# Retention and a gated MLP on one core: the first two blocks re-ordered

## The chip, the core and the metric

The kernel runs on one core of one Trainium2 chip. A core has five engines with queues of their own, each in program order: TensorE (PE, matrix products), VectorE (DVE), ScalarE (ACT), GpSimd (POOL) and SyncE (SP, which here only issues DMAs). They wait for each other through semaphores. PE writes to PSUM, which has eight banks of 128 partitions x 512 float32. The metric is the device time of one execution, in microseconds (us), median of several runs.

## What is computed

```python
# q, k, v: (8 batches, 8 heads, 576 positions, 64)
scores = q @ k^T / sqrt(64)
Dmat   = gamma_h ** (i - j) for i >= j, else 0      # gamma_h = 1 - 2**(-5-h)
attn   = (scores * Dmat) @ v
x      = attn, as 4608 tokens x 512                  # 8 * 576 tokens
h      = x @ w_in                                    # 512 x 2048
g      = h * cos(h)
out    = g @ w_out                                   # 2048 x 512, float32
```

## The kernel before

The attention is done per batch in five chunks r = 0..4 of 128 positions (the last has 64), the MLP in nine blocks j of 512 tokens. Batches have 576 tokens and blocks 512, so block 0 lies wholly in batch 0, and block 1 takes batch 0's last 64 tokens and the first 448 of batch 1.

**One chunk.** Three loads on SP's queue bring k, q and v (256 KB each; 128 KB in the last chunk) into float32 tiles kn, qn, vn. There is one set of these tiles, so the load of batch b+1's chunk r waits until the casts of batch b's chunk r have read them. The casts make bf16: `kcast` copies k, `decay` multiplies q and v by powers of gamma. `turn` transposes k and q by four matmuls each against the identity, into a PSUM bank, and ACT copies the bank to the tile kqt (L286). From batch 2 on `prep_dma` does the casts on POOL and the transposition by a DMA on SP instead. `scores` multiplies (banks sc0 and sc1), and DVE applies the mask (L325). `rest` gives the chunk's output in bank po and the running state in bank st, and ACT copies po to the token store xt (L367) and st to sb (L371).

**One block.** `mlp1(j, dt, o0, n)` computes 128 columns of the first layer for n tokens: four matmuls into one of four banks mm0 to mm3, taken in turn by `bank`; ACT takes the cosine as a shifted sine (L389), DVE multiplies (L392) into the tile gt. `mlp2(j, st, part)` does a quarter of the second layer's contraction for 128 tokens; after four parts ACT copies the bank to one of three float32 buffers osb (L414), and a DMA on SP stores it (L416). An osb buffer is written again only when its store has landed.

**Order.** The order of each queue is the order in which `emit` writes the calls. SP loads chunks 0 to 3 of batch 0. POOL issues the four loads of w_in (each 512 KB as stored in bf16), the first three held until q of chunk 1, 2 and 3 has landed, then four loads of w_out; SP's load of chunk 4 is held until the second of w_in has landed. In batch 0 ACT casts k, DVE decays q and POOL decays v, behind its weight loads. `idle` issues matmuls on a zero tile. Block 0's first layer is done partly in groups of 256 tokens, as chunks come. Then, for each block, the second layer's sixteen calls run with token tile st outside and part inside, so that one bank finishes every fourth call; between them stand the rest and the scores of the next batch, and in block 0 also the casts and turns of batch 1 with the loads of batch 2. From block 1 on, the first layer runs with `prep_dma` of batch j+1 between its groups, each followed by the loads of batch j+2.

## Time and profile before

| | us |
|---|---|
| runs | 338.02, 337.24, 331.56 (median 337.24) |
| the profiled execution | 334.09 |
| its span, first to last instruction | 332.4 |
| PE busy | 302.3 (91%) |
| ACT busy | 182.8 (55%) |
| DVE busy | 152.2 (46%) |
| POOL busy | 105.4 (32%) |

### The profile page before, as it was taken

How to read it: one execution, taken by the hardware profiler on the slowest of the kernel's cores; microseconds unless marked ns; L12 is line 12 of the kernel's file. 1: busy time of each engine (PE TensorE's matmuls, PEld its weight loads, DVE VectorE, ACT ScalarE, POOL GpSimd, SP SyncE). 2: the span in 40 equal slices, each digit the busy share in tenths (PEclk: the TensorE clock that was granted, in tenths of full speed). 3: DMA queues.
4: the chain of work that ended last, by engine and by line, in shares of the span. 5: the costliest groups of instructions: out<-in, count | busy, mean ns of one | idle time of the engine just before them, and what ended most of it. 6: DMA issues, size and time to landing. Idle time of an engine off the chain costs nothing.

```text
span 332.4 us, 5974 instructions
## 1 busy us (share of the span) xinstructions
PE 302.3 (91%) x2271; PEld 154.7 (47%) x2310; DVE 152.2 (46%) x244; ACT 182.8 (55%) x336; POOL 105.4 (32%) x125
## 2 busy tenths in 40 slices
PE   6219669999999999999999999999999999999996
PEld 2106444555445445544554455445544554444442
DVE  2205457334843574357335833574367427604710
ACT  8206677566734773477347744764376447625721
POOL 1272177763546064506540535055400000000000
PEclk9756799999999999999999999999999999999999
DMA  9999999986996599569946995799480100011002
GB/s 170 225 209 194 211 207 198 230 195 144 221 201 173 126 219 201 162 133 233 193 140 150 204 196 150 163 213 190 133 165 10 64 33 32 4 63 63 2 37 89
DMA packets 150556, 49.41 MB, mean 149 GB/s; under 512 B 141824, under 2 KB 145920, under 8 KB 150528
## 3 DMA queue, kind: packets, MB, share of 16 engines
q1 hardware_dynamic: 146304, 44.84, 64.6%
q0 software_dynamic: 4224, 4.19, 7.6%
q8 instruction: 18, 0.29, 0.4%
q14 instruction: 10, 0.08, 0.1%
HBM read 36.70 MB, written 9.44 MB: 139 GB/s over the span
## 4 chain that ended last, share of the span: by engine, by line
PE 89%; SPq 3%; DMA 2%; issue 2%; POOL 2%; ACT 2%; DVE 0%; ACTq 0%
PE mm L300 57%; PE mm L302 20%; PE po L300 6%; PE sc L300 4%; SPq L225 3%; DMA qn<-in_q_dram 2%; PE st L300 1%; POOL wout L238 1%; POOL win L231 0%; ACT xt L367 0%; ACT osb L414 0%; ACT kqt L286 0%; POOL vb L253 0%; DVE kq L253 0%; ACT sb L371 0%
## 5 line engine op out<-in xcount | busy, mean ns | idle before, releaser
L392 DVE TENSOR_TENSOR gt<-mm,cb 128x512 bf16<-128x512 f32 (+1 forms) x152 | 100.5, 664 | 61.6 <-ACT cb L389 60.3
L300 PE MATMUL mm<-xt,win 128*128 128x512 bf16 (+1 forms) x443 | 116.1, 371 | 1.1 <-ACT xt L367 0.6
L389 ACT ACTIVATE cb<-mm,c_pih 128x512 bf16<-128x512 f32 (+1 forms) x152 | 100.6, 665 | 29.6 <-PE mm L302 29.0
L300 PE MATMUL mm<-wout,gt 128*128 128x512 bf16 x407 | 111.6, 380 | 2.6 <-issue 2.5
L325 DVE TENSOR_TENSOR rt<-sc,mk 128x512 bf16<-128x512 f32 (+1 forms) x80 | 47.2, 631 | 99.0 <-PE sc L302 99.0
L300 PEld LDWEIGHTS mm<-xt,win 128*128 128x128 bf16 x456 | 44.7, 99 | 50.4 <-ACT xt L367 0.7
L300 PEld LDWEIGHTS mm<-wout,gt 128*128 128x128 bf16 x432 | 39.0, 98 | 45.1 <-issue 0.4
L302 PE MATMUL mm<-xt,win 128*128 128x512 bf16 (+1 forms) x152 | 56.4, 371 | 0.4
L302 PE MATMUL mm<-wout,gt 128*128 128x512 bf16 x144 | 54.6, 379 | 0.5
L367 ACT ACTIVATE xt<-po 128x512 bf16<-128x512 f32 (+1 forms) x40 | 22.2, 555 | 57.1 <-PE po L302 57.0
L414 ACT ACTIVATE osb<-mm 128x512 f32<-128x512 f32 x36 | 21.5, 597 | 51.7 <-PE mm L302 51.7
L246 POOL CAST kq<-kn 128x512 bf16<-128x512 f32 (+1 forms) x35 | 21.3, 610 | 80.7 <-DMA kn<-in_k_dram 69.5
L253 POOL TENSOR_TENSOR vb<-vn,wv 128x512 bf16<-128x512 f32 (+1 forms) x40 | 41.9, 1054 | 12.6 <-DMA vn<-in_v_dram 12.2
L253 POOL TENSOR_TENSOR kq<-qn,uq 128x512 bf16<-128x512 f32 (+1 forms) x35 | 36.5, 1042 | 22.6 <-DMA qn<-in_q_dram 22.6
L300 PE MATMUL po<-rt,vb 128*64 128x128 bf16 (+1 forms) x280 | 16.1, 225 | 12.8 <-POOL vb L253 12.8
L371 ACT ACTIVATE sb<-st 64x256 bf16<-64x256 f32 x64 | 23.9, 373 | 0.8
L302 PEld LDWEIGHTS mm<-xt,win 128*128 128x128 bf16 x152 | 15.0, 99 | 16.4
L302 PEld LDWEIGHTS mm<-wout,gt 128*128 128x128 bf16 x144 | 14.1, 98 | 17.0
L300 PEld LDWEIGHTS po<-rt,vb 128*64 128x64 bf16 (+1 forms) x280 | 9.8, 110 | 18.9 <-POOL vb L253 13.0
L300 PE MATMUL sc<-kqt 64*128 64x128 bf16 (+1 forms) x280 | 15.7, 221 | 1.9 <-ACT kqt L286 1.9
L286 ACT ACTIVATE kqt<-mm 128x512 bf16<-128x512 f32 (+1 forms) x20 | 10.3, 553 | 6.8 <-PE mm L302 6.6
L300 PEld LDWEIGHTS po<-kqt,sb 128*128 128x128 bf16 x128 | 9.6, 100 | 6.9
(40 smaller groups left out, 122.9 us busy)
## 6 DMA issues: line engine op xcount, KB each, us to landing
out_dram<-osb SPq DMA_DIRECT2D x36, 256.0 KB, 2.2
kn<-in_k_dram SPq DMA_DIRECT2D x32, 256.0 KB, 4.0
qn<-in_q_dram SPq DMA_DIRECT2D x32, 256.0 KB, 4.6
vn<-in_v_dram SPq DMA_DIRECT2D x32, 256.0 KB, 4.7
win<-in_moe_w_in_dram POOLq DMA_DIRECT2D x4, 512.0 KB, 7.2
wout<-in_moe_w_out_dram POOLq DMA_DIRECT2D x4, 512.0 KB, 15.4
kn<-in_k_dram SPq DMA_DIRECT2D x8, 128.0 KB, 3.1
qn<-in_q_dram SPq DMA_DIRECT2D x8, 128.0 KB, 3.7
```

Of the source, the lines that this page charges most:

```text
L225: return self.s.dma("sp", f"{x}n{r}", lambda e: e.dma_start(dst, src), writes=[bt], after=after)
L246: fn = (lambda e: e.activation(o, x, AF.Copy)) if eng == "act" else (lambda e: e.tensor_copy(o, x))
L253: self.s.op(eng, lambda e: e.tensor_tensor(bass.AP(t, off, [[pitch, ck], [D_, H_], [1, D_]]), bass.AP(self.ST32[x][r], 0, [[DM, ck], [D_, ...
L286: fn = (lambda e: e.activation(o, p, AF.Copy)) if eng == "act" else (lambda e: e.tensor_copy(o, p))
L300: self.nc.tensor.matmul(o, a, b, **kw)
L302: return s.done("pe", self.nc.tensor.matmul(o, a, b, **kw), reads, writes)
L325: s.op("dve", lambda e: e.tensor_tensor(bass.AP(self.RT[r % 2][hp], 0, p3), bass.AP(self.SC[hp], 0, p3), bass.AP(self.MK, 0, [[CH, ck], [0 ...
L367: fn = (lambda e: e.activation(o, p, AF.Copy)) if xeng == "act" else (lambda e: e.tensor_copy(o, p))
L371: s.op("act", lambda e: e.activation(bass.AP(self.SB[r % 2], 64 * hp * 512 + 64 * hp, [[512, 64], [128, NP], [1, D_]]), bass.AP(self.ST, 6 ...
L389: s.op("act", lambda e: e.activation(ci, mi, AF.Sin, bias=self.C_PIH.ap(), scale=1.0), reads=[bm, self.bC], writes=[bcb])
L392: s.op("dve", lambda e: e.tensor_tensor(bass.AP(g, dt * TB + o0, [[16 * TB, 128], [1, n]]), mi, ci, ALU.mult), reads=[bm, bcb], writes=[bg])
L414: s.op("act", lambda e: e.activation(o.ap(), m.ap(), AF.Copy), reads=[bm], writes=[bo])
```

## The change

Batch 0's casts: k on ACT, q and v on DVE. SP loads all five chunks of batch 0 at once. POOL's weight loads are held for k of chunk 2 and of chunk 3; only two of w_out's four loads stand ahead, the other two behind POOL's casts of batch 1's chunk 0. Chunk 4's scores and rest stand within block 0's first layer. All casts of batch 1, each with the loads of batch 2, stand ahead of block 0's second layer. That layer runs with part outside and token tile inside, in the four mm banks at once, and batch 1's turns then use the banks sc0 and sc1. Block 1's first layer runs in three strips of 192, 128 and 192 tokens, with batch 1's remaining turns, scores and rests and batch 2's `prep_dma` between the groups.

```diff
-    def turn(self, b, r, x, eng):
+    def turn(self, b, r, x, eng, sc=None):
...
-        m, bm = self.bank()
+        m, bm = self.bank() if sc is None else (self.SC[sc], self.bSC[sc])
...
-    def mlp2(self, j, st, part):
+    def mlp2(self, j, st, part, wide=False):
...
-        if part == 0:
-            self.m2 = self.bank()
-        m, bm = self.m2
+        if wide:
+            m, bm = self.MM[st], self.bMM[st]
+        else:
+            if part == 0:
+                self.m2 = self.bank()
+            m, bm = self.m2
...
+    def cast_pe(self, b, r, k, q, v):
+        self.kcast(k, b, r)
+        self.decay(q, "q", b, r)
+        self.decay(v, "v", b, r)
+        for x in "kqv":
+            self.load(x, b + 1, r)
+
     def emit(self):
...
-        land = [[self.load(x, 0, r) for x in "kqv"] for r in range(4)]
+        land = [[self.load(x, 0, r) for x in "kqv"] for r in range(NCH)]
         self.consts()
-        w = [self.w_in_load(i, after=[land[1][1]] if i == 0 else [land[2][1]] if i == 1 else [land[3][1]] if i == 2 else ()) for i in range(NWI)]
-        for x in "kqv":
-            self.load(x, 0, 4, after=[w[1]] if x == "k" else ())
-        for i in range(NWO):
-            self.w_out_load(i)
...
+        self.w_in_load(0, after=[land[2][0]])
+        self.w_in_load(1, after=[land[3][0]])
+        self.w_in_load(2)
+        self.w_in_load(3)
+        self.w_out_load(0)
+        self.w_out_load(1)
+
+        def turn0(r):
+            self.cast_pe(0, r, "act", "dve", "dve")
+            self.turn(0, r, "k", "act")
+            self.turn(0, r, "q", "act")
+
+        def turn1(r):
+            self.turn(1, r, "k", "act", 0)
+            self.turn(1, r, "q", "act", 1)
+
+        self.idle(12)
+        turn0(0)
         self.scores(0, 0)
-        self.idle(4)
-        prep_pe(0, 1)
+        turn0(1)
         self.rest(0, 0)
         self.scores(0, 1)
-        self.idle(4)
-        prep_pe(0, 2)
+        turn0(2)
         self.rest(0, 1)
         self.scores(0, 2)
-        self.idle(4)
+        self.idle(6)
         for dt in range(4):
             self.mlp1(0, dt, 0, 256)
...
         for dt in range(8):
             self.mlp1(0, dt, 256, 256)
-        prep_pe(0, 4)
-        for dt in range(8, 16):
+        for dt in range(8, 12):
             self.mlp1(0, dt)
+        turn0(4)
+        self.scores(0, 4)
+        for dt in range(12, 16):
+            self.mlp1(0, dt)
+        self.rest(0, 4)
+
+        for r in range(NCH):
+            self.cast_pe(1, r, "pool", "pool", "pool")
+            if r == 0:
+                self.w_out_load(2)
+                self.w_out_load(3)
+        parts = [(st, part) for part in range(4) for st in range(4)]
+        for n, (st, part) in enumerate(parts):
+            if n == 8:
+                turn1(0)
+            if n == 10:
+                self.scores(1, 0)
+            if n == 13:
+                turn1(1)
+            if n == 15:
+                self.rest(1, 0)
+                self.scores(1, 1)
+            self.mlp2(0, st, part, True)
+        for dt in range(16):
+            self.mlp1(1, dt, 0, 192)
+            if dt == 4:
+                self.rest(1, 1)
+            if dt == 8:
+                turn1(2)
+            if dt == 12:
+                self.scores(1, 2)
+        self.rest(1, 2)
+        turn1(3)
+        for dt in range(16):
+            self.mlp1(1, dt, 192, 128)
+            if dt == 3:
+                self.scores(1, 3)
             if dt == 9:
-                self.scores(0, 4)
-        for j in range(NTB):
-            if j:
+                self.rest(1, 3)
+        turn1(4)
+        for dt in range(16):
+            self.mlp1(1, dt, 320, 192)
+            if dt % 3 == 2:
+                self.prep_dma(2, dt // 3)
+            if dt == 4:
+                self.scores(1, 4)
+        for j in range(1, NTB):
+            if j > 1:
                 for dt in range(16):
                     self.mlp1(j, dt)
-                    if 1 <= j and j + 1 < B_ and dt % 3 == 2:
+                    if j + 1 < B_ and dt % 3 == 2:
                         self.prep_dma(j + 1, dt // 3)
+            b = j + 1
             for n in range(16):
-                b = j + 1
-                if b == 1 and n % 3 == 0 and n < 15:
-                    prep_pe(1, n // 3)
```

More of the change, by code (lines that the diff above doesn't have):

```diff
@@ L417, in mlp2 @@
             bass.AP(self.out, row0 * DM, [[DM, 128], [1, DM]]), o.ap()), reads=[bo])
+    def cast_pe(self, b, r, k, q, v):
[4 more added lines that the diff above has]
+            self.load(x, b + 1, r)
     def emit(self):
         s = self.s
-        land = [[self.load(x, 0, r) for x in "kqv"] for r in range(4)]
+        land = [[self.load(x, 0, r) for x in "kqv"] for r in range(NCH)]
         self.consts()
-        w = [self.w_in_load(i, after=[land[1][1]] if i == 0 else [land[2][1]] if i == 1 else [land[3][1]] if i == 2 else ()) for i in range(NWI)]
-        for x in "kqv":
-            self.load(x, 0, 4, after=[w[1]] if x == "k" else ())
-        for i in range(NWO):
-            self.w_out_load(i)
-        def prep_pe(b, r):
-            self.kcast("act" if b == 0 else "pool", b, r)
-            self.decay("dve" if b == 0 else "pool", "q", b, r)
-            self.decay("pool", "v", b, r)
-            self.turn(b, r, "k", "act")
-            self.turn(b, r, "q", "act")
-            for x in "kqv":
-                self.load(x, b + 1, r)
-        self.idle(10)
-        prep_pe(0, 0)
+        self.w_in_load(0, after=[land[2][0]])
[13 more added lines that the diff above has]
+        turn0(0)
         self.scores(0, 0)
-        self.idle(4)
-        prep_pe(0, 1)
+        turn0(1)
         self.rest(0, 0)
         self.scores(0, 1)
-        self.idle(4)
-        prep_pe(0, 2)
+        turn0(2)
         self.rest(0, 1)
         self.scores(0, 2)
-        self.idle(4)
+        self.idle(6)
         for dt in range(4):
@@ L454, in emit @@
         self.rest(0, 2)
-        prep_pe(0, 3)
+        turn0(3)
         self.scores(0, 3)
```

## The prediction

> **What bounds the kernel now.** I read the page's slices first: where is TensorE (PE) not full?

> ```profile
> PE   6219669999999999999999999999999999999996
> PEclk9756799999999999999999999999999999999999
> DMA  9999999986996599569946995799480100011002
> ```

> One slice is 8.3 us. After the sixth slice (50 us) PE is at nine tenths or more to the end; all that can be won lies ahead of it. There the DMA engines are full. The chain of waits says what held PE:

> ```profile
> 10.98 7.20 DMA qn<-in_q_dram
> 18.47 1.48 POOL win L231 x2
> 19.95 0.66 POOL wout L238
> 20.67 2.25 POOL wout L238 x3
> 22.92 1.08 POOL vb L253
> ```

> GpSimd (POOL) waits for q of chunk 3, issues six weight loads, and only then decays v of chunk 0; the list of waits shows PE idle 12.8 us for it, up to 24.05. The timeline then gives the first first-layer group at 30.66, the first second-layer group at 56.51, and the first group of block 1 at 77.74, from where PE runs full. So I judge the change by when block 1's first layer ends: before, with PE's last first-layer group, 91.55.

> The timeline of SyncE (SP) shows what I expect to decide:

> ```profile
> 57.03 1.84 SPq L225 DMA_DIRECT2D kn<-in_k_dram  x1
> 58.96 1.09 SPq L225 DMA_DIRECT2D qn<-in_q_dram  x1
> 60.15 1.09 SPq L225 DMA_DIRECT2D vn<-in_v_dram  x1
> 62.03 0.36 SPq L416 DMA_DIRECT2D out_dram<-osb  x1
> ```

> Block 0's first store is queued behind the loads of batch 2's chunks 0 and 1 only. The v load issued at 60.15 landed 4.6 us later (64.7), the store 3.4 us after issue (65.4): in order. Early on, issues are 1.1 us each, the pace of landings, with four loads in flight: SP itself is held by full queues.

> **The front: idle matmuls, casts, weights.** Batch 0's v decay goes from POOL (1.04 us) to VectorE (DVE; its q decay, the same shape, 0.68 to 0.69, 1.09 when POOL ran beside it): five instructions, 3.4 us of DVE, under an engine busy 0.8 of 10 us in 10:20. Chunk 0's v landed at 6.4, so the 12.8 us wait goes. Next late is w_in 0: issued when k of chunk 2 lands (11.3 before, from issue 6.10 and 5.2 to landing), 6.8 to 7.8 from issue to landing by the same load before: 18.1 to 19. The two removed idle(4)s are dead time either way; idle(6) and the two idle matmuls more at the start run while PE waits, cost nothing. Before, first layer to second layer took 56.5-30.7 = 25.8 us, of which some 3 was PE waiting for chunk 3 (34 to 37) and 2.8 for chunk 4's turn (45.8 to 48.6). The latter goes, since chunk 4's loads no longer wait for w_in 1 (k, q, v landed 29.2, 33.7, 36.8) and the turn stands further back. So the second layer can start at 18.5+25.8-3 to -6, plus 0.6 for rest(0,4): 39 to 42, against 56.5.

> **The second layer by quarters.** 16 groups at 0.864 (start to start) are 13.8 us; two turns (0.9 each), two scores (0.35), one rest (0.8) lie among them: 17.1, so it ends at about 57. w_out 2 and 3 now stand on POOL behind batch 1's chunk 0 casts, 0.61+1.04+1.04, whose data lands about 38.5 (before 43.9, with 1.05 MB of w_out ahead of it that now comes later, at 0.2 MB/us). Issued 41, landed 46 to 50, needed 47 and 51: 0 to 3 us late. That is covered by what comes next.

> **The stores.** By quarters all four banks finish within 3 us, and there are three osb buffers. The fourth eviction waits on ScalarE (ACT) for the first store to land; behind it in ACT's queue stand all the Sin of block 1, and PE can do one group of block 1 (bank 2) before it needs the bank that this eviction frees. And the first store is now issued behind *all* loads of batch 2, because the five cast_pe(1, r) with their loads stand ahead of the second layer on SP. So the stall ends when those loads have landed, whatever the front gained. By 64.7 before had moved batches 0 and 1 (3.54 MB each), the weights (4.19, as stored) and two chunks (1.57). Batch 2's other 2.5 chunks are 1.97 MB at 217 GB/s (10:12 and 12:14 in the windows): 9.1 us, so 73.8. Less about 1 us, as the queues ran thin before between 42 and 56 (DMA share 0.78 in 42:44 against 1.35 in 6:8), plus 0.7 for the store, as above: landed about 73.5, eviction done (0.60) at 74.2. Bounds 72 (faster, full queues) and 76 (casts of batch 1 leave gaps). PE idles some 17 us, and resumes at block 1's second group; before, that group began at 78.60. So 4.4 us of the front's 20 us is left.

> **Strips.** Block 1's first layer becomes 48 groups for 16. On PE nothing: 64 times (192+128+192) columns is the same streaming, 13.8 us. On ACT: the 128x256 Sin is 0.47 alone, 0.39 back to back (1.57 for 4); 128x512 is 0.69, so 0.86 ns per column; I estimate 0.335 for 192 and 0.28 for 128 back to back, 32x0.335+16x0.28 = 15.2 us. [...] To these come what before did during block 0's second layer and is now among the strips: three rests (0.49+0.77 of ACT, 3.8 us), two turns (1.08 each) and a half one (0.87): 22 us of ACT, against 18.6 of PE (13.8, 3x0.8, 3x0.35, 2x0.45, 0.3) and 17.7 of DVE (0.32 and 0.26 by the same reckoning, masks 3.3). ACT becomes the bound of this stretch, with some 8% lost to banks and masks.

> **The clock.** After the first stall the granted clock was 0.50 for 6.0 us of work (24.05 to 30.1); after the short gap at 36, for 3.4. A 17 us stall brings this back. I take 4.7 us: PE does 192-column groups in 0.66 then, ACT idles some 1.8 us. [...]

> **Sum.** 73.5 + 0.6 + 4.7 (2.9 of ACT's 22 done) + 19.1x1.08 = 99.4, less 0.9, since PE goes on to the next layer ahead of ACT's last Sin: 98.5, against 91.55: +7. With everything from there on as before, and prep_dma(2)'s transposes covered (issued on SP at 75 to 80, batch 2 landed, first needed at 100), the profiled run, 334.09 with a span of 332.4, becomes 341. That run lies 3 us under the median of 337.24, whose counterpart is 344; I give 342.5, between. Bounds: ACT perfectly packed with short cold time, 20 us, and 72: 92.5, +1; 27 us and 76: 103, +11.

> **Rivals.**
> *The first store gets out early (faster).* Place: SP's queue. If it landed before block 0's second layer is done (57), the strips would start there: 57+24.5 = 81.5, ten less than 91.55: 324 on the profile, 327 on the median. It decides below a landing at 62 (over 2% faster). For it: POOL is free early and SP's first issues take 0.44. Against: the program order, and 14.8 MB that cannot land by then. Chance 0.08.
> *The stall is there, the strips are cheaper.* ACT and PE interleave well, 20 to 23 us: +1 to +6, 335 to 343. For it: four first-layer groups of 256 needed only 0.44 each at 42 to 45. Chance 0.34.
> *Forecast:* stall and strips as summed, +6 to +9. Chance 0.40.
> *Strips or weights worse.* Latency per bank (matmul, Sin, multiply: 0.5+0.42+0.35 and three handovers, over four banks) and masks between push the strips to 27 us, or DMA gaps the landing to 77: +9 to +13, 343 to 351. Chance 0.15.
> *The front doesn't speed up*, because w_in comes late: up to 17 us of it is swallowed by the same wait, so the number is the forecast's. Chance 0.03 of its being later still.

> **How the numbers follow.** 2% is 6.7 us, about what a measurement of this kernel tells from no change (its three runs spread over 331.56 to 338.02). Slower by more: half of the forecast's case and more (0.30), the worse ones (0.18): 0.48, with the median's basis 0.50. Within: 0.40. Faster by more: 0.08, and 0.02 for baseline scatter, 0.10. The range takes the cheap and the dear strips on both bases: 332 to 351.

> **What would show it.** PE's first group of the first layer at about 18.5; second layer from 39 to 42; then PE idle from about 57 to 74, ACT's fourth osb activation waiting on the store, its wait the longest in the trace; on SP all 15 loads of batch 2 ahead of the first store, issued about 69; clock at 0.5 for 3 to 7 us after; ACT the fuller engine of the strips; last first-layer group of block 1 at 95 to 102. Wrong: a store landing before 65, or PE running through from 57.

## The result and the profile after

The changed kernel takes 346.02 us (median; 345.65 to 346.34), the kernel before 336.56 (331.56 to 338.02) beside it: a ratio of 1.037, 95% interval 1.025 to 1.048. It is slower. The ratio, like all below, leaves out runs over 1.5% slower than the fastest of the same kernel, here 337.24 and 338.02; with them it would be 1.028. The profiled execution took 346.0, with a span of 344.3: 11.9 us more than the one of before.

The page's slices of the changed kernel, 8.6 us each, in tenths (PEclk is the granted PE clock):

```profile
PE   6669699519689999999999999999999999999996
PEclk9588989858999999999999999999999999999999
DMA  9999999999980159948992998399753010011002
```

PE's hole at 10 to 24 us is gone, and there is a new one in the eighth and ninth slices. PE's timeline there:

```profile
64.19 0.41 PE L300 MATMUL mm<-xt,win 128*128 128x192 bf16 x3
64.44 0.25 PE L302 MATMUL mm<-xt,win 128*128 128x192 bf16 x1
76.28 0.66 PE L300 MATMUL mm<-xt,win 128*128 128x192 bf16 x3 [11.60 <-ACT osb L418]
```

One group of block 1 runs, and the second waits 11.6 us for an eviction. ACT's timeline (the four evictions, that is the copies to osb, and the first Sin of block 1 behind them):

```profile
60.45 0.60 ACT L418 ACTIVATE osb<-mm 128x512 f32<-128x512 f32 x1 [3.89 <-PE mm L302]
...
61.90 1.32 ACT L418 ACTIVATE osb<-mm 128x512 f32<-128x512 f32 x2
...
75.63 0.60 ACT L418 ACTIVATE osb<-mm 128x512 f32<-128x512 f32 x1 [11.26 <-DMA out_dram<-osb]
76.12 0.41 ACT L389 ACTIVATE cb<-mm,c_pih 128x192 bf16<-128x192 f32 x1
```

The fourth waits for the first one's store. SP's timeline says why that is late:

```profile
70.06 0.60 SPq L225 DMA_DIRECT2D qn<-in_q_dram  x1
70.76 0.59 SPq L225 DMA_DIRECT2D vn<-in_v_dram  x1
71.41 5.18 SPq L420 DMA_DIRECT2D out_dram<-osb  x4
```

The buffer was full at 61.05. Its store is issued at 71.41, directly behind the last load of batch 2, and lands 4.1 us later (the row takes all four stores together). From 54.5 to 71.4 no wait of SP for an engine shows; its loads were issued about one a microsecond, and between 64.4 and 76.3 the DMA engines were full (share 1.11, 233 GB/s). The chain of waits of the changed kernel goes the same way:

```profile
70.76 0.59 SPq L225
...
71.41 4.14 DMA out_dram<-osb
...
75.63 0.61 ACT osb L418
...
76.28 0.66 PE mm L300 x3
```

PE's first group of each stage, from the timelines of both kernels:

| starts at, us | before | after | difference |
|---|---|---|---|
| block 0, first layer | 30.66 | 19.43 | -11.2 |
| block 0, second layer | 56.51 | 47.89 | -8.6 |
| block 1, first layer | 77.74 | 64.19 | -13.6 |
| block 1, second layer | 91.55 | 103.47 | +11.9 |

So all is lost within block 1's first layer: 39.3 us for 13.8. Of these 25.5 us more, 11.6 are the wait; the rest is for the experiments.

### The profile page after: what moved, and what is told of

It is laid out like the page before. It is cut to its first block, busy times and chain, and to the rows that moved or that the text cites. A ratio compares the mean times of both kernels' runs of the same rounds, so it can differ in the third digit from the quotient of the medians.

```text
span 344.3 us, 6389 instructions
## 1 busy us (share of the span) xinstructions
PE 312.0 (91%) x2434; PEld 164.2 (48%) x2434; DVE 159.2 (46%) x281; ACT 187.4 (54%) x368; POOL 100.0 (29%) x120
## 3 DMA queue, kind: packets, MB, share of 16 engines
q0 software_dynamic: 4224, 4.19, 7.5%
## 4 chain that ended last, share of the span: by engine, by line
PE 80%; ACT 6%; DVE 4%; SPq 4%; DMA 3%; issue 1%; POOL 1%; ACTq 0%; POOLq 0%
PE mm L300 53%; PE mm L302 17%; PE po L300 6%; SPq L225 4%; PE sc L300 4%; DVE gt L392 2%; ACT cb L389 2%; DMA qn<-in_q_dram 2%; DVE rt L325 1%; ACT kqt L286 1%; DMA out_dram<-osb 1%; PE st L300 1%; DVE kq L253 1%; ACT sb L371 1%; ACT xt L367 1%
## 5 line engine op out<-in xcount | busy, mean ns | idle before, releaser
L392 DVE TENSOR_TENSOR gt<-mm,cb 128x512 bf16<-128x512 f32 (+3 forms) x184 | 104.1, 575 | 81.5 <-ACT cb L389 80.0
L300 PE MATMUL mm<-xt,win 128*128 128x512 bf16 (+3 forms) x552 | 124.3, 341 | 15.5 <-ACT osb L418 11.6
L389 ACT ACTIVATE cb<-mm,c_pih 128x512 bf16<-128x512 f32 (+3 forms) x184 | 106.2, 596 | 33.8 <-PE mm L302 32.0
L300 PE MATMUL mm<-wout,gt 128*128 128x512 bf16 x432 | 117.1, 380 | 0.3 <-issue 0.2
L300 PEld LDWEIGHTS mm<-xt,win 128*128 128x128 bf16 x552 | 51.8, 100 | 62.8 <-ACT osb L418 11.8
L302 PE MATMUL mm<-xt,win 128*128 128x512 bf16 (+3 forms) x184 | 62.8, 341 | 0.0
L300 PEld LDWEIGHTS mm<-wout,gt 128*128 128x128 bf16 x432 | 39.3, 98 | 45.9 <-ACT xt L367 0.6
L302 PE MATMUL mm<-wout,gt 128*128 128x512 bf16 x144 | 54.6, 379 | 0.0
L253 POOL TENSOR_TENSOR kq<-qn,uq 128x512 bf16<-128x512 f32 (+1 forms) x35 | 36.5, 1043 | 27.6 <-DMA qn<-in_q_dram 27.1
L253 POOL TENSOR_TENSOR vb<-vn,wv 128x512 bf16<-128x512 f32 (+1 forms) x35 | 36.5, 1042 | 5.4 <-PE po L302 2.9
L302 PEld LDWEIGHTS mm<-xt,win 128*128 128x128 bf16 x184 | 18.5, 101 | 14.9 <-issue 0.6
L302 PEld LDWEIGHTS mm<-wout,gt 128*128 128x128 bf16 x144 | 14.1, 98 | 17.0
L300 PE MATMUL po<-rt,vb 128*64 128x128 bf16 (+1 forms) x280 | 16.3, 227 | 0.0
L300 PE MATMUL po<-kqt,sb 128*128 128x128 bf16 (+1 forms) x128 | 12.2, 221 | 0.9 <-DVE rt L325 0.9
## 6 DMA issues: line engine op xcount, KB each, us to landing
wout<-in_moe_w_out_dram POOLq DMA_DIRECT2D x4, 512.0 KB, 13.6
```

Source lines behind the costliest of these rows:

```text
L253: self.s.op(eng, lambda e: e.tensor_tensor(bass.AP(t, off, [[pitch, ck], [D_, H_], [1, D_]]), bass.AP(self.ST32[x][r], 0, [[DM, ck], [D_, ...
L300: self.nc.tensor.matmul(o, a, b, **kw)
L302: return s.done("pe", self.nc.tensor.matmul(o, a, b, **kw), reads, writes)
L389: s.op("act", lambda e: e.activation(ci, mi, AF.Sin, bias=self.C_PIH.ap(), scale=1.0), reads=[bm, self.bC], writes=[bcb])
L392: s.op("dve", lambda e: e.tensor_tensor(bass.AP(g, dt * TB + o0, [[16 * TB, 128], [1, n]]), mi, ci, ALU.mult), reads=[bm, bcb], writes=[bg])
```

## The experiments

Ratios are to the kernel of before, run beside each.

**A fourth buffer.**

```diff
-        self.NOSB = 3
+        self.NOSB = 4
```

> The changed kernel with a fourth osb buffer, so that the fourth eviction waits for no store. Theory (the wait for the first store is the loss): PE goes on at 64.7 us instead of 76.3, and the clock stays up, which was 0.5 from 76.3 to 80.2 and cost about 1.7 us: 346.0 - 11.6 - 1.7 = 333 us, a little under the 336.6 of before; the stores still land only from 75 us on. Rival (the strips or batch 1's data hold PE there anyway): another wait shows between 64 and 76 and the time stays at 340 us or more.

331.98 us, ratio 0.996 (0.992 to 1.000). ACT's timeline of this kernel:

```profile
63.54 0.77 ACT L371 ACTIVATE sb<-st 64x256 bf16<-64x256 f32 x2
64.33 0.60 ACT L418 ACTIVATE osb<-mm 128x512 f32<-128x512 f32 x1
64.83 0.42 ACT L389 ACTIVATE cb<-mm,c_pih 128x192 bf16<-128x192 f32 x1
```

The fourth eviction follows the state copies with no wait, while the stores are issued only at 72.45. Fourteen microseconds (346.02 less 331.98) hang on one buffer of 256 KB, and the kernel is then level with before, or a little ahead. The theory's number was 333.

**The stores ahead of batch 2's loads,** three buffers:

```diff
 def cast_pe(self, b, r, k, q, v):
...
-        for x in "kqv":
-            self.load(x, b + 1, r)
+        if b == 0:
+            for x in "kqv":
+                self.load(x, b + 1, r)
...
             self.mlp2(0, st, part, True)
+        for r in range(NCH):
+            for x in "kqv":
+                self.load(x, 2, r)
```

> The changed kernel, three osb buffers, but the fifteen loads of batch 2 stand behind block 0's four stores on SP's queue. Theory (the order on SP's queue delays the store, not a lack of DMA bandwidth as such): the first store is issued at about 61 us and lands by 64, the fourth eviction hardly waits, the time is that of four_buffers within 2 us, 332 to 336 us; batch 2's loads start at 64 and have landed by 82, in time for the third strip. Rival (the DMA engines are full whatever the order): the store lands after 68 us and the time stays above 339 us.

332.78 us, ratio 0.998 (0.994 to 1.001). SP's timeline of this kernel:

```profile
60.72 4.27 SPq L420 DMA_DIRECT2D out_dram<-osb  x4
```

And ACT's, with the fourth eviction:

```profile
63.24 0.77 ACT L371 ACTIVATE sb<-st 64x256 bf16<-64x256 f32 x2
64.04 0.60 ACT L418 ACTIVATE osb<-mm 128x512 f32<-128x512 f32 x1
```

The store goes out as soon as its buffer is full (60.70), and the fourth eviction starts at 64.04 without a wait. The buffers are as few as in the changed kernel and the bytes the same: it is the place on SP's queue that made the store late.

**The front of before with the rest of the change.** From the five `cast_pe(1, r)` on this is the changed kernel (w_out's loads all stand ahead), and before them the kernel of before; the diff has the core.

```diff
-        land = [[self.load(x, 0, r) for x in "kqv"] for r in range(NCH)]
+        land = [[self.load(x, 0, r) for x in "kqv"] for r in range(4)]
...
-        self.w_out_load(0)
-        self.w_out_load(1)
+        for i in range(NWO):
+            self.w_out_load(i)
...
-            self.cast_pe(0, r, "act", "dve", "dve")
+            self.kcast("act" if b == 0 else "pool", b, r)
+            self.decay("dve" if b == 0 else "pool", "q", b, r)
+            self.decay("pool", "v", b, r)
```

> Block 0's first layer and all ahead of it as before, from there on the changed kernel (casts of batch 1 with the loads of batch 2 ahead of the second layer, quarters, three osb buffers, strips). Theory (the end of the wait is set by the landing of batch 2's loads, whatever the front gained): the second layer starts 9 us later than in the changed kernel, at 57 us, and ends at 73 to 74; the fourth eviction still comes at 75 to 77; the time is the changed kernel's 346 us within 2. Rival (the front's gain was kept, and the wait moves with it): 9 us more, 354 to 356 us.

343.89 us, ratio 1.030 (1.024 to 1.035). The second layer starts at 56.25, 8.4 us later than in the changed kernel, and the kernel is not slower. PE's timeline:

```profile
72.34 0.41 PE L300 MATMUL mm<-xt,win 128*128 128x192 bf16 x3
...
74.89 0.42 PE L300 MATMUL mm<-xt,win 128*128 128x192 bf16 x3 [2.06 <-ACT osb L418]
```

The fourth eviction comes at 74.24 (75 to 77 was expected), 1.4 us earlier than in the changed kernel. The wait has shrunk from 11.6 to 2.1 us, and its end has moved by no more than that, and not later: it is the loads that set it, and an earlier front only waits longer.

By the ratios, 1.030 and 1.037, the intervals overlap. In the traces block 1's second layer starts 3.1 us earlier here (100.41 for 103.47): 1.4 are the earlier end of the wait, and 1.7 come from the clock. After the long wait it is at half, after the short one it is not. These are windows over the same work, four groups and a rest, in the changed kernel and then in this one, with the granted clock third from the end of the row:

```profile
76.30:80.20 3.90, 3.90 (x37) 3.50 (x38) 1.79 (x5) 2.06 (x6) 0.41 (x1) 0.50 0.69 163
```

```profile
74.90:77.00 2.10, 2.10 (x36) 1.96 (x36) 1.45 (x5) 1.72 (x6) 0.56 (x1) 1.00 0.62 175
```

From the second group of block 1 to its second layer it takes 27.2 us in the changed kernel (76.28 to 103.47) and 25.5 here (74.89 to 100.41).

**The strips alone,** in the kernel of before:

```diff
-            if j:
+            if j == 1:
+                for dt in range(16):
+                    self.mlp1(1, dt, 0, 192)
+                    if dt % 3 == 2:
+                        self.prep_dma(2, dt // 3)
+                for dt in range(16):
+                    self.mlp1(1, dt, 192, 128)
+                for dt in range(16):
+                    self.mlp1(1, dt, 320, 192)
+            elif j:
```

> The kernel of before, with only block 1's first layer cut into strips of 192, 128 and 192 tokens; nothing stands among the strips but batch 2's casts and transposes, as before. Theory (a bank's way through matmul, Sin and multiply paces groups this small: 0.375 us and 0.316 us a group): 17.1 us for 13.8, the time 3 us longer than before. Rival (PE paces them, 4 x 192 columns being 0.33 us and 4 x 128 0.22 us): 14 us, no difference; then what the strips lost in the changed kernel is due to the turns, scores and rests among them.

338.58 us, ratio 1.013 (1.007 to 1.019). The layer takes 17.8 us (79.11 to 96.94) instead of 13.8; the theory's 17.1 is near, the rival's 14 is not. Is it also the theory's cause? A window within the strips, with the columns PE, PEld, DVE, ACT and POOL after the length:

```profile
85.00:91.00 6.00, 5.95 (x73) 4.29 (x71) 5.47 (x19) 5.99 (x19) 3.31 (x4) 1.00 1.18 231
```

ACT is busy 5.99 of 6.00 us, which looks like the bound. It is not, for its Sin can come faster. Here the 16 groups of 128 tokens come every 0.327 us. In the changed kernel, where the matmuls were done and Sin stood queued, three started at 89.62, 89.87 and 90.12, 0.25 us apart:

```profile
89.62 0.89 ACT L389 ACTIVATE cb<-mm,c_pih 128x128 bf16<-128x128 f32 x3
```

What paces the groups is the way of a bank. Lines of strips_alone, from five narrow windows, follow one bank from its matmuls to its next ones, four groups later:

```profile
85.36 0.33 PE L300 MATMUL mm<-xt,win 128*128 128x128 bf16 x3
85.53 0.22 PE L302 MATMUL mm<-xt,win 128*128 128x128 bf16 x1
...
85.83 0.37 ACT L389 ACTIVATE cb<-mm,c_pih 128x128 bf16<-128x128 f32 x1
...
86.23 0.29 DVE L392 TENSOR_TENSOR gt<-mm,cb 128x128 bf16<-128x128 f32 x1
...
86.67 0.33 PE L300 MATMUL mm<-xt,win 128*128 128x128 bf16 x3
```

The Sin starts 0.09 us after the last matmul (whose end is modelled), the multiply 0.03 after the Sin, and PE takes the bank again 0.15 after the multiply. It is so for all 40 groups from the ninth on, but for one Sin that comes 0.05 later. One round is 1.31 us, over four banks 0.327 a group; for 192 tokens it is 1.53, 0.384 a group. That makes 17.5 us for the 48 groups. PE by itself would need less: four matmuls of 128 columns came every 0.22 us elsewhere (a turn in late_front, 68.40 and 68.62). So the theory holds in its cause too, as far as a trace can show it; no run changed the number of banks.

**Two strips of 256:** the same edit with `self.mlp1(1, dt, 0, 256)` and `self.mlp1(1, dt, 256, 256)`.

> The kernel of before, with only block 1's first layer cut into two strips of 256 tokens instead of three of 192, 128 and 192. Theory (ACT paces the strips: in strips_alone its Sin came without a gap, 0.327 us each for 128 columns and 0.38 for 192, against 0.22 and 0.33 on PE): 32 Sin of 0.39 to 0.43 us are 12.5 to 13.8 us, no more than PE's 13.8, so 0 to 0.5 us over before. Rival (every cut costs, by switching strips or by the extra weight loads on PE): half of the three strips' loss and more, 2 us or more over before.

334.37 us, ratio 1.001 (0.998 to 1.005); the layer takes 14.1 us (78.58 to 92.68). The expectation took ACT for the pace, by the busy row above. The run doesn't tell that from the way of a bank, which forecasts the same: its round for 256 tokens is 1.76 us, over four banks 0.44 a group, and PE does a group in 0.44 as well (the first four, whose banks were free, start at 78.58, 79.02, 79.46 and 79.89). So cutting cost the layer 0.3 us here, where a bank's round, shared by the four banks, was no longer than PE's group (0.44 us both), and 4.0 us in strips_alone, where it was longer (0.327 for 0.22 with 128 tokens, 0.384 for 0.33 with 192).

**The front alone.** The changed kernel to the end of block 0's first layer, then the kernel of before.

```diff
         self.w_out_load(1)
+        self.w_out_load(2)
+        self.w_out_load(3)
...
         self.rest(0, 4)
...
-        for r in range(NCH):
-            self.cast_pe(1, r, "pool", "pool", "pool")
...
-        for j in range(1, NTB):
-            if j > 1:
+        for j in range(NTB):
+            if j:
                 for dt in range(16):
                     self.mlp1(j, dt)
...
             for n in range(16):
+                b = j + 1
+                if b == 1 and n % 3 == 0 and n < 15:
+                    self.cast_pe(1, n // 3, "pool", "pool", "pool")
+                    self.turn(1, n // 3, "k", "act")
+                    self.turn(1, n // 3, "q", "act")
```

> The changed kernel up to the end of block 0's first layer, with all four loads of w_out ahead, and from there on the kernel of before (second layer by token tile, batch 1's casts and turns among it, block 1's first layer in groups of 512). Theory (the front gains by itself, and the rest gave it back): the second layer starts at 47 to 48 us instead of 56.5, 8 us are kept, 328 us. Rival (block 0's second layer is then held by batch 1's chunks, which cannot land before 44 to 57 us): 3 to 5 us kept, 332 to 334 us.

323.80 us, ratio 0.970 (0.966 to 0.974): faster than both kernels. The second layer starts at 45.52 and block 1's first layer at 66.26, 11.5 us earlier than before. The theory had 8 us and 328. With all loads of w_out ahead the second layer starts 2.4 us earlier than in the changed kernel; the experiment with w_out below bears on that.

**The quarters alone,** on top of that: a fourth buffer, `self.mlp2(0, n % 4, n // 4, True)` in block 0, and batch 1's turns in the score banks.

> front_alone with block 0's second layer by quarters in four banks, a fourth osb buffer, and batch 1's turns in the score banks; batch 1's loads and casts and block 1's first layer as in front_alone. Theory (the quarters cost nothing but the crowding of the four evictions): front_alone's 323.8 us within 1.5. Rival (the turns in the score banks hold up the scores): 2 us or more over front_alone, with PE waiting for masks or kqt between 45 and 68 us.

324.04 us, ratio 0.971 (0.966 to 0.975): the same. The order by quarters, with a fourth buffer, costs nothing by itself, and gains nothing.

**Chunk 4 earlier.** In the changed kernel PE stopped between 37.9 and 42 us for chunk 4's turn, which I had taken to be gone. This is front_alone with chunk 4's casts and turns put forward:

```diff
             self.mlp1(0, dt, 0, 256)
+        self.cast_pe(0, 4, "act", "dve", "dve")
         self.rest(0, 3)
         for dt in range(8):
             self.mlp1(0, dt, 256, 256)
-        for dt in range(8, 12):
-            self.mlp1(0, dt)
-        turn0(4)
-        self.scores(0, 4)
-        for dt in range(12, 16):
+        self.turn(0, 4, "k", "act", 0)
+        self.turn(0, 4, "q", "act", 1)
+        for dt in range(8, 16):
             self.mlp1(0, dt)
+            if dt == 10:
+                self.scores(0, 4)
```

> front_alone with chunk 4's casts moved ahead of chunk 3's rest (its v lands at about 27 us) and its two turns, into the score banks, ahead of the second eight groups of 512. Theory (PE's waits at 37.8 to 41 us are the Sin queue ahead of chunk 4's casts, and the turn's round trips): about 2.5 us less than front_alone, 321 us. Rival (the casts wait for v of chunk 4 on DVE and hold up the groups ahead): the wait appears near 29 us instead, and the time is front_alone's.

323.98 us, ratio 0.969 (0.964 to 0.974): nothing gained. The wait is gone (the second layer starts at 43.99, 1.5 us earlier), yet block 1's first layer starts at 66.34 as in front_alone. The time is the rival's, the place is not: PE now waits for POOL's casts of batch 1 instead (0.28, 0.33 and 0.81 us, between 43 and 49), whose data is not there earlier.

**w_out in one piece,** in the kernel with four buffers:

```diff
         self.w_out_load(1)
+        self.w_out_load(2)
+        self.w_out_load(3)
...
-            if r == 0:
-                self.w_out_load(2)
-                self.w_out_load(3)
```

> four_buffers with all four loads of w_out ahead of batch 1's casts on POOL, instead of two ahead and two behind. Theory (the split let batch 1's chunk 0 land early, so that POOL's casts fell on DVE's decays of chunk 4, 1.48 and 1.09 us for 0.68 each, and PE's clock dropped): the decays take 0.68 us again, the second layer starts at 45 to 46 us instead of 48.2, and 1.5 to 2.5 us of that are kept: 330 us. Rival (what is gained there is lost to batch 1's later chunks, which then hold the turns of the second layer): four_buffers' 332 us within 1.

331.32 us, ratio 0.993 (0.990 to 0.996), beside 0.996 (0.992 to 1.000) for four_buffers: the medians don't tell them apart, and whether the front's gain is kept stays open. That the decays are faster the traces show. DVE's timeline of the changed kernel, then of this one, for chunk 4's q and v:

```profile
39.51 1.48 DVE L253 TENSOR_TENSOR kq<-qn,uq 64x512 bf16<-64x512 f32 x1
40.92 1.09 DVE L253 TENSOR_TENSOR vb<-vn,wv 64x512 bf16<-64x512 f32 x1
```

```profile
38.84 0.67 DVE L253 TENSOR_TENSOR kq<-qn,uq 64x512 bf16<-64x512 f32 x1
39.44 0.68 DVE L253 TENSOR_TENSOR vb<-vn,wv 64x512 bf16<-64x512 f32 x1
```

In the changed kernel POOL decays batch 1's chunk 0 at the same time (38.41 and 39.41, 1.04 each) and then issues two loads of w_out (40.40 to 41.96); here its decay starts at 40.21. In four_buffers itself the two took 1.55 and 1.09. The second layer starts at 45.11 instead of 48.21 in four_buffers and block 1's second layer 2.3 us earlier (88.45 for 90.75); the two profiled executions took 330.76 and 333.03.

**All together:** front_quarters with chunk 4 early.

> front_quarters (no strips, quarters, four osb buffers, loads of batch 2 among the second layer) with chunk 4's casts and turns early as in front_early4. Theory (the front's end no longer matters, batch 1's chunks now set the end of block 0's second layer): 323 to 324.5 us, that of front_alone. Rival (by quarters, what front_early4 lost to waits for batch 1 is won): 321 to 322 us.

324.69 us, ratio 0.973 (0.969 to 0.976). The second layer starts at 42.41, and PE waits 1.39 and 0.99 us for POOL's casts in it: the theory holds, and POOL itself waits for batch 1's loads there (3.44 us for v of chunk 0). front_alone stays the version to keep.

## Why the prediction was right, and where it was not

The direction and the mechanism were right: the store behind batch 2's loads, the fourth eviction behind the store, block 1 behind the eviction. Two edits that touch nothing else, a buffer and an order, each take the loss away, and moving the front 8.4 us later doesn't move the end of the wait later. The measured 346.0 lies within the range of 332 to 351. On the profiled executions the loss was 11.9 us and not 7, which is the case given 0.15, "strips or weights worse"; the strips were worse, and the weights were not.

- **The landing.** Forecast: store issued at about 69, landed 73.5. Measured: 71.4 and 75.5. Short by 2.0; my bound was 76. The rate was not it: from 48 to 72 the DMA engines moved 213 GB/s on average, and the sum took 217. Where the 2.0 were lost was not traced.
- **The strips.** Forecast 24.3 us from the eviction's end (74.2) to the next layer (98.5); measured 27.2 (76.28 to 103.47). Short by 2.9. The term that was mis-sized is "some 8% lost to banks and masks", 1.5 us. Two windows of the changed kernel end with block 1's last Sin; one begins at the end of the stretch at half clock, the other at the eviction's end (ACT's busy time is the fourth after the length):

```profile
80.20:104.15 23.95, 19.00 (x266) 15.85 (x265) 15.41 (x48) 20.36 (x58) 12.39 (x14) 0.99 1.00 184
76.23:104.15 27.92, 22.91 (x300) 19.37 (x301) 17.20 (x53) 22.49 (x63) 12.88 (x15) 0.92 0.95 181
```

  ACT is busy 22.5 us for the 22 of the forecast, but after the half clock it is idle for 3.6 of 24.0 us. The rival named what runs there: a bank's way, and the masks. PE waits 1.01 and 1.04 us for multiplies that stand behind masks on DVE, 0.89 for a mask and 0.90 for a copy to kqt. Sin back to back was not the short term. Where Sin were queued in the changed kernel, they started every 0.25 us for 128 columns (89.62, 89.87), 0.30 for 192 (81.67, 81.97) and 0.36 for 256 (33.34, 33.70), and the forecast had 0.28, 0.335 and 0.39 (1.57 for 4 is an average that takes in the whole of the last one). What a bank's way, the masks and the copies each took in this mix no run tells apart.
- **The clock.** Forecast 4.7 us at half, measured 3.9, within the rows' 3.4 to 6.0. Its price, 1.7 us by late_front, where the same work took 2.1 us, agrees with the 1.8 us of idle ACT in the 3.9.
- **The front.** Forecast: second layer at 39 to 42. Measured 47.9. The step that failed is "the latter goes", chunk 4's turn. Its loads were not the cause: v of chunk 4 had landed at 26.9 (issued at 15.43, 11.5 us), 12 us before the first of its casts. The casts stand behind the Sin of four groups on ACT and behind their multiplies on DVE, and each of the two turns is a round trip that PE waits for (1.34, 1.32 and 0.47 us). Beside POOL's casts, put forward by the change itself, and its issue of w_out 2 and 3, DVE was slow too (1.48 and 1.09 us for chunk 4's two decays, 0.67 and 0.68 in w_out_ahead), and the granted clock fell to half (0.56, 0.50 and 0.50 in the three us from 43). The wait for chunk 3, which the lower bound took away as well, stayed as it was before to the hundredth (1.89 and 0.95 us). From the first layer to the second it took 28.5 us, and 25.8 before. It cost the total nothing, as forecast: the store's wait swallowed it.
- **The front's idle matmuls, the v decay on DVE and the first weight load** went as forecast: first group at 19.4 for 18.5, no wait for v.
- **w_out 2 and 3** were issued at 40.4 for 41, and no wait of PE for them shows between 48 and 64; the cover was not needed.
- **The second layer by quarters:** forecast 17.1 us, measured 16.3.

The rival of a front that doesn't speed up fell: the front brings 10 us in front_alone, where each store stands behind the loads of one or two chunks only and block 1 waits for no store. That the number still lies in the range owes something to its width: it had been opened to 351 for dear strips.

What stays open: in four_buffers block 1's first layer with the turns, scores and rests among the strips takes 26.6 us, 8.8 more than the strips alone, of which PE's own share by the sum is about 4.7 (the prediction's terms add up to 18.5, not 18.6, less 13.8). How the other 4 divide between masks on DVE and copies on ACT was not tried. Nor was a strip with more banks, or a store issued from a queue that carries no loads.

## What to carry to other kernels

When outputs are finished close together, count the buffers that they leave through and look at what stands ahead of their stores on the queue: prefetches put there earlier were paid for here by the engine that waits for the buffer (ACT, 11.3 us), and by all that is queued behind it (PE, 11.6). Before cutting a layer into smaller groups, add up a bank's way through all engines, handovers included, and divide by the number of banks; in these runs cutting was all but free where that was no longer than a group's matmuls (0.44 us both), and not where it was longer (0.327 for 0.22). An engine that shows no gap need not be the bound, as ACT was not, busy for 5.99 of 6.00 us with a Sin every 0.327: see whether its instructions can come faster where they are queued (0.25). And a gain at the front is real only if the next fixed point, here the landing of a batch, moves with it: delay the front on purpose and see whether the end moves (8.4 us later here, and the wait's end 1.4 earlier).

## What the runs showed of the hardware

VectorE's decay, a multiply of two SBUF inputs over 512 columns, took 0.67 to 0.69 us with GpSimd idle or all but idle, in the kernels before and after and in w_out_ahead. In the kernel before, it took 0.85 us (26.69) where GpSimd's decay ended 0.28 us into it, and 1.09 (46.98) beside two of GpSimd's. In the changed kernel chunk 4's first took 1.48 us (39.51) beside GpSimd's decay and its issue of w_out's loads, and the second 1.09 (40.92) beside that issue. Of GpSimd's decays beside them, that of the changed kernel took 1.04 us, and the two in the kernel before 1.04 and 1.32. Why VectorE's took longer no run tells.

A Sin from PSUM to bfloat16, 128 partitions, took 0.37 us for 128 columns, 0.42 for 192 and 0.47 for 256 in the changed kernel (89.62, 81.35 and 32.97), and several in a queue started 0.25, 0.30 and 0.36 us apart.

The runs of the changed kernel lie within 0.7 us, those of before within 6.5. In the kernels with the front of before, block 0's first layer began at 30.14, 30.64, 30.66 and 33.14 us in four traces (strips_alone, late_front, before, two_strips); in the changed kernel everything then waits for the same landing. That this evens the runs out is my reading; it was not tried.
